# Layer two's mixing: P1 as seven half-depth products, and block sums on GpSimd instead of DMA

## The chip, the cores and the metric

The kernel runs on one core of one Trainium2 chip. The metric is the device time of the whole program in microseconds, the median of several runs of one build. An engine-by-engine profile of one execution stands beside it. The engines are called as in the profile: PE (TensorE, with its weight loads as PEld), DVE (VectorE), ACT (ScalarE), POOL (GpSimd), SP (SyncE, which here only issues DMAs).

## The reference

Four blocks follow each other on a 2048 x 512 activation, each with a layernorm in front and a residual around it: attention, mixer, attention, mixer, all with the same two sets of weights. Attention and the first mixer are called layer one here, the other two layer two. The change lies in the mixer's mixing over the sequence:

```python
def _B_ref(x, w_in, w_sp, b_sp, w_out):      # x: 1 x 2048 x 512, float32
    z = _gelu(jnp.einsum("bsd,df->bsf", x, w_in))      # 2048 x 1792
    z1 = z[..., :Fh]                                   # Fh = 896
    z2 = _layernorm(z[..., Fh:], axis=-1)
    g = jnp.einsum("ts,bsf->btf", w_sp, z2) + b_sp[None, :, None]   # w_sp: 2048 x 2048
    return jnp.einsum("bsf,fd->bsd", z1 * g, w_out)
...
x = x + _A_ref(_layernorm(x, axis=-1), A_wqkv, A_wo)
x = x + _B_ref(_layernorm(x, axis=-1), B_w_in, B_w_sp, B_b_sp, B_w_out)
x = x + _A_ref(_layernorm(x, axis=-1), A_wqkv, A_wo)
x = x + _B_ref(_layernorm(x, axis=-1), B_w_in, B_w_sp, B_b_sp, B_w_out)
```

`w_sp` is the same in both layers, so sums of its blocks that layer one makes can be kept in device memory for layer two.

## The kernel before

**Precision.** Each float32 matrix is split into a high part (`h`, rounded by ACT to the format that PE multiplies) and a low part (`l`, the difference, made by DVE). A product is three matmuls: high by high, high by low, low by high.

**The mixing as seven products.** `g` is computed as a product of 2 x 2 blocks in seven block products instead of eight. Class `P4` does them in the order `P2, P1, P6, P7, P4, P5, P3`. A plain product runs over `k` = 0 to 7; each step takes one tile of 128 x 2 x 512 of the spatial weights (or of a sum of blocks of them), and does 24 matmuls of 128 x 512. A product named in `DIVIDED` for its layer (index 0 is layer one) is itself done as seven products of half depth: 14 steps (`k` = 0 to 13, `SEVEN` gives the order), each of 12 matmuls of 128 x 512. Before the change layer one divides P2 and P4, layer two P2, P4 and P5.

**One step.** For step `g`, `fetch` loads the raw weights from DRAM, five steps ahead, into half a `qd` tile (`Halves` hands those out). `wsp` lets ACT write the high part into a `qd` tile `w` (line 1695), and DVE the low part (line 1698, 128 x 1024 elements); there are six `qd` tiles for both uses. `zsp` (plain) or `zsum` and `zpart` (divided) prepare the z side on ACT and DVE. The weights are made two steps ahead of `mm`, which issues the matmuls. In a divided product `evac_div` adds the finished PSUM banks into the gate tiles `gb` (`unit(n, f)` is 128 x 512 of them) on DVE after every second step (line 1870); in a plain one `evac` does it at the end. Each engine works through its own instructions in the order in which the program writes them; semaphores join the engines. What stands in the program's loop

```python
self.sp(g + 2)
self.zahead(g + (3 if p == "P5" else 4))
self.mm(g)
```

therefore sets the order on every engine. `gate` multiplies finished units by `z1`, part of them on POOL (line 1961). In layer two the low parts of P5 and of half of P7 are not made anew: layer one stores them (`KEPT`), and POOL's queue loads them.

**Sums of weight blocks.** Products of sums need sums of blocks of `w_sp`. `Sums` makes the first level (`s1`, `s`) on POOL during layer one (line 1604); eight of these additions fall into layer one's P1. The second level, for divided products, lies in DRAM tiles `halves[p, m, q]`, with m from 1 to 4. For P2 the sums are made by DVE and POOL; for P4 and P5 by DMA: `halve` copies one block from DRAM to DRAM (SP's queue) and then adds another onto it by an accumulating DMA (POOL's queue, line 1572). P5's copies are issued in layer one's P3 (`PARTS`), its additions in layer one's output stage and in layer two's attention.

**The z side of P1 in layer two.** Column sums of z for P6, P7 and later products, `a[:, H2]`, are made by DVE in `zsp` while P1 runs (lines 1735 and 1736, 128 x 384 each, for 8 tiles).

Of the kernel before, what the change touches and what calls it, by code (L numbers as in the profile page):

```python
# [10 lines left out]
F32 = mybir.dt.float32  # L11
# [84 lines left out]
DIVIDED = ("P2", "P4"), ("P2", "P4", "P5")  # L96
# [17 lines left out]
PARTS |= {("P7", k): 12 + k for k in range(4)} | {("P3", k): 16 + k for k in range(8)}  # L114
# [38 lines left out]
def mixer_kernel(ctx: ExitStack, tc: tile.TileContext, x_in, wqkv, wo_d, win1_d, win2_d, wsp_d, bsp_d, wout_d,  # L153
# [299 lines left out]
    class P1:  # L453
# [1075 lines left out]
    class Sums:  # L1529
# [3 lines left out]
        def __init__(self):  # L1533
# [8 lines left out]
            self.parts, self.halves = [], {}  # L1542
# [4 lines left out]
            self.parts = [(what, p, m, q) for p in ("P4", "P5")[:len(DIVIDED[1]) - 1] for what in ("copy", "add") for m in (1, 3, 2, 4)  # L1547
                          for q in range(2)]
# [7 lines left out]
        def halve(self, n, after, i=None):  # L1556

            if not 0 <= n < len(self.parts):
                return
            what, p, m, q = self.parts[n]  # L1560
            row = 2 if p == "P2" else 0
            j, s = {1: ((1, 0), (1, 4)), 3: ((0, 0), (1, 0)), 2: ((0, 0), None), 4: ((0, 4), None)}[m][what == "add"] or (0, 0)
            src = self.s1[j, s + 2 * q:s + 2 * q + 2] if p == "P5" else wsp_d[row + j, HT + s + 2 * q:HT + s + 2 * q + 2]
            if what == "copy":
                nc.sync.dma_start(self.halves[p, m, q], src)
            else:
                if m in (2, 4):
                    src = self.halves[p, m // 2, q]
                dst = self.halves[p, m, q]
                if i is not None:  # L1570
                    dst, src = dst[i:i + 1], src[i:i + 1]
                d = nc.gpsimd.dma_start(dst, src, accum_op=OP.add, max_dma_last_dim=4096)
                if after is not None:
                    behind(d, after)
# [53 lines left out]
    class P4:  # L1628
# [8 lines left out]
        def __init__(self, p2, sums):  # L1637
# [17 lines left out]
            self.halves, self.fetched = Halves(quads), 0  # L1655

# [5 lines left out]

        def fetch1(self, g):
            p, k = self.steps[g]
            t = self.halves.get()
            if p in self.div:
                r, q = self.SEVEN[k // 2], k % 2
                j, s = {1: (0, 0), 2: (0, 4), 4: (1, 4)}.get(r, (0, 0))
                if r in (1, 2, 4):
                    s += 2 * q  # L1670
                    ap = self.sums.s1[j, s:s + 2] if p == "P5" else wsp_d[(2 if p == "P2" else 0) + j, HT + s:HT + s + 2]
# [18 lines left out]
        def wsp(self, g):  # L1690
# [6 lines left out]
            if at is None or not self.L:  # L1697
                nc.vector.tensor_sub(w[:, 1], r, w[:, 0].bitcast(F32))  # L1698
            if at is not None:
                if self.L:  # L1700
                    nc.gpsimd.dma_start(w[:, 1], at)
                else:
                    nc.sync.dma_start(at, w[:, 1].bitcast(F32))
            self.halves.put(r)
            if g == len(self.steps) - 1:
                self.halves.close()
            self.w[g] = w

        def kept(self, g):
# [3 lines left out]
            if p not in self.div:  # L1713
                t = self.sums.lows[p][:, k]
# [8 lines left out]
        def zsp(self, g):  # L1723
            p, k = self.steps[g]
            H1, H2, H3 = self.H1, self.H2, self.H3
# [41 lines left out]

        def zdiv(self, p, half, side, q, i):
            return ztile[(0 if p == "P5" else HT) + 4 * half + 2 * q + i][:, 256 * side:256 * side + 256]
# [79 lines left out]
        def evac_div(self, p, r):  # L1849
# [4 lines left out]
            for f in range(2):  # L1854
# [6 lines left out]
                n, f = (2 + j if p == "P2" else j), 2 * half + f  # L1861
# [9 lines left out]
            if r in (2, 3, 4):  # L1871
                b = self.bank.pop(name)
                if p != "P5":
# [8 lines left out]
        def carry(self, j):  # L1882
# [3 lines left out]
            nc.scalar.activation(b, self.unit(j, 6), AF.Copy, scale=-1.0)  # L1886
# [77 lines left out]
        def evac(self, p, js=(0, 1)):  # L1964
# [3 lines left out]
            for j in js:  # L1968
                a, b = 2 + j, j
                for f in range(3):  # L1970
# [6 lines left out]
                    elif p == "P6":  # L1977
                        V.tensor_add(self.unit(a, 4 + f), q, bs[a])
                    elif p == "P7":
                        V.tensor_sub(self.unit(b, 4 + f), bs[b], q)  # L1980
# [182 lines left out]
        def out7(self, nxt):  # L2163
# [5 lines left out]
            for j in range(HT):  # L2169
# [76 lines left out]
        def run(self, nxt):  # L2246
# [33 lines left out]
            for g in range(n):  # L2280
# [7 lines left out]
                self.mm(g)  # L2288
                if evac_first:
# [10 lines left out]
                if p in self.div:  # L2300
# [3 lines left out]
                    if k % 2 == 1:  # L2304
                        self.evac_div(p, self.SEVEN[k // 2])
                    if div_first:
# [3 lines left out]
                    if p == "P5":  # L2310
                        if k > 10 and k < 13:
                            self.carry(12 - k)
# [99 lines left out]
```

## Time and profile before

| | |
|---|---|
| median of 3 runs | 1345.41 us (1345.4 to 1346.75) |
| span of the profiled execution, first to last instruction | 1345.0 us |
| PE busy | 1338.2 us, 99% |
| DVE busy | 1043.7 us, 78% |
| ACT busy | 726.6 us, 54% |
| POOL busy | 462.6 us, 34% |
| layer one's P1, P5 on PE | about 385 to 429 us, 532 to 575 us |
| layer two's P2, P1 on PE | 1013 to 1052 us, 1052 to 1095 us |

The profile gives one execution; its span leaves out what lies around the first and the last instruction, so the profiled execution's own time is its span of 1345.0 us and a little more, and the runs' median is 0.4 us above it. A row of the order of time reads: start, length, engine, line, operation, output <- inputs, shapes, count, and in brackets the idle time before it with what ended it. A tile's name without its number: `qd` are weights, `pg` pages of 128 x 512, `bank` is PSUM, `bg` the gate tiles, `z_z` the z tiles. In rows of waits stand the waiting instruction, what it waited for, total us, times, longest. In groups stand count | busy us, mean ns | idle us before.

### The profile page before, as it was taken

Reading aid. Unit: us, or ns where it says so; the run is one execution under the profiler, and the core shown is the slowest. Engines: PE = TensorE matmul, PEld = TensorE weight load, DVE = VectorE, ACT = ScalarE, POOL = GpSimd, SP = SyncE. Lnnn points to the kernel's source line nnn. Section 1 sums busy time; section 2 is a strip of 40 time slices with the busy share of each in tenths; the row PEclk is TensorE's granted clock in tenths of the full one; section 3 lists DMA queues with packets and bytes.
Section 4 is the critical chain, followed back from the end, with each engine's and each line's share of the span. In section 5 each row is a group of like instructions: output and inputs, shape, how many; then the busy total and the mean of one; then the engine's idle time right before and its main releaser. Section 6 shows DMA issues by size and latency. Waiting matters only on the chain.

```text
span 1345.0 us, 19202 instructions
## 1 busy us (share of the span) xinstructions
PE 1338.2 (99%) x6538; PEld 1141.4 (85%) x6538; DVE 1043.7 (78%) x1662; ACT 726.6 (54%) x1219; POOL 462.6 (34%) x613
## 2 busy tenths in 40 slices
PE   9999999999999999999999999999999999999998
PEld 7888888888888888889988888888888888888898
DVE  7679877763797789888867777778689858899885
ACT  5774534334643264445677755557677433666454
POOL 3755675544022300301425543544531012121021
PEclk9999999999999999999999999999999999999999
DMA  5897477877877986884867652678777445579343
GB/s 184 279 318 272 164 262 254 293 270 258 298 236 256 285 265 203 293 306 80 179 172 230 173 133 89 208 238 272 217 206 231 168 168 178 177 241 313 122 79 64
DMA packets 172403, 290.30 MB, mean 216 GB/s; under 512 B 14480, under 2 KB 53904, under 8 KB 172048
## 3 DMA queue, kind: packets, MB, share of 16 engines
q1 hardware_dynamic: 154192, 251.58, 55.5%
q0 software_dynamic: 18112, 37.49, 13.0%
q8 instruction: 51, 0.84, 0.2%
q14 instruction: 48, 0.39, 0.1%
HBM read 204.08 MB, written 101.71 MB: 227 GB/s over the span
## 4 chain that ended last, share of the span: by engine, by line
PE 96%; DMA 1%; DVE 1%; ACT 1%; SPq 0%; issue 0%; POOL 0%; DVEq 0%
PE bank L228 14%; PE bank L230 14%; PE bank L229 13%; PE bank L1920 12%; PE bank L1921 12%; PE bank L1922 12%; PE bank L2118 3%; PE bank L2119 3%; PE bank L2120 3%; PE bank L986 1%; PE bank L988 1%; PE bank L987 1%; DMA pg<-yt 1%; PE bank L384 1%; PE bank L2132 1%; PE bank L2131 1%
## 5 line engine op out<-in xcount | busy, mean ns | idle before, releaser
L1921 PE MATMUL bank<-qd,pg 128*128 128x512 f32 x736 | 286.5, 389 | 0.0
L1920 PE MATMUL bank<-qd,pg 128*128 128x512 f32 x736 | 286.4, 389 | 0.0
L1922 PE MATMUL bank<-qd,pg 128*128 128x512 f32 x736 | 286.3, 389 | 0.0
L1695 ACT ACTIVATE qd<-qd 128x1024 fp32r<-128x1024 f32 x142 | 149.4, 1053 | 127.3 <-PE bank L1922 107.0
L1698 DVE TENSOR_TENSOR qd<-qd,qd 128x1024 fp32r<-128x1024 f32 x132 | 169.2, 1284 | 52.6 <-ACT qd L1695 41.7
L230 PE MATMUL bank<-qd,pg 128*128 128x512 f32 x448 | 174.6, 390 | 0.0
L1921 PEld LDWEIGHTS bank<-qd,pg 128*128 128x128 f32 x736 | 138.2, 188 | 28.9 <-DVE qd L1698 0.3
L1920 PEld LDWEIGHTS bank<-qd,pg 128*128 128x128 f32 x736 | 138.2, 188 | 28.7 <-DVE bg L1870 0.2
L1922 PEld LDWEIGHTS bank<-qd,pg 128*128 128x128 f32 x736 | 138.2, 188 | 28.7
L228 PE MATMUL bank<-qd,pg 128*128 128x512 f32 x308 | 120.6, 392 | 0.3 <-DVE pg L217 0.3
L1961 POOL TENSOR_TENSOR bg<-bg,pg 128x512 f32<-128x512 f32 x28 | 45.7, 1632 | 218.1 <-ACT qd L1695 99.4
L229 PE MATMUL bank<-qd,pg 128*128 128x512 f32 x308 | 120.1, 390 | 0.0
L230 PEld LDWEIGHTS bank<-qd,pg 128*128 128x128 f32 x448 | 84.1, 188 | 17.8 <-DVE pg L217 0.2
L363 POOL TENSOR_SCALAR rs<-mv 128x1 f32<-128x1 f32 x80 | 25.1, 314 | 190.0 <-DVE mv L361 181.0
L372 ACT ACTIVATE pg<-pg,nb,rs 128x512 f32<-128x512 f32 x52 | 42.2, 812 | 85.5 <-POOL nb L366 79.3
L1604 POOL TENSOR_TENSOR pg<-pg,pg 128x512 f32<-128x512 f32 x48 | 68.0, 1417 | 59.2 <-DMA pg<-in_wsp_dram 57.3
L214 ACT ACTIVATE pg<-pg 128x512 fp32r<-128x512 f32 x85 | 53.0, 624 | 61.7 <-DVE pg L1789 18.4
L2120 PE MATMUL bank<-wo,qd 128*128 128x256 f32 x288 | 81.4, 283 | 0.0
L2118 PE MATMUL bank<-wo,qd 128*128 128x256 f32 x276 | 78.2, 283 | 0.0
L2119 PE MATMUL bank<-wo,qd 128*128 128x256 f32 x276 | 78.0, 283 | 0.0
L228 PEld LDWEIGHTS bank<-qd,pg 128*128 128x128 f32 x308 | 57.9, 188 | 12.5 <-DVE pg L217 0.7
L229 PEld LDWEIGHTS bank<-qd,pg 128*128 128x128 f32 x308 | 58.0, 188 | 12.1 <-DVE qd L217 0.2
(276 smaller groups left out, 3278.6 us busy)
## 6 DMA issues: line engine op xcount, KB each, us to landing
qd<-s SPq DMA_DIRECT2D x62, 512.0 KB, 4.2
qd<-in_wsp_dram SPq DMA_DIRECT2D x40, 512.0 KB, 4.1
qd<-hP SPq DMA_DIRECT2D x40, 512.0 KB, 4.7
pg<-z SPq DMA_DIRECT2D x56, 256.0 KB, 4.9
pg<-in_wsp_dram SPq DMA_DIRECT2D x52, 256.0 KB, 4.3
s<-pg SPq DMA_DIRECT2D x48, 256.0 KB, 3.7
z<-pg SPq DMA_DIRECT2D x40, 256.0 KB, 3.3
pg<-w POOLq DMA_DIRECT2D x38, 256.0 KB, 4.6
```

What stands on the lines that cost most here:

```text
L228: nc.tensor.matmul(out, ah, bh, start=start, stop=False)
L229: nc.tensor.matmul(out, ah, bl, start=False, stop=False)
L230: nc.tensor.matmul(out, al, bh, start=False, stop=stop)
L1604: nc.gpsimd.tensor_tensor(t, a, b, op=OP.add)
L1695: self.mark = nc.scalar.activation(w[:, 0], r, AF.Copy)
L1698: nc.vector.tensor_sub(w[:, 1], r, w[:, 0].bitcast(F32))
L1920: m(out, h[:, o], w[:, 0, j, :], start=start, stop=False, skip_group_check=True)
L1921: m(out, h[:, o], w[:, 1, j, :], start=False, stop=False, skip_group_check=True)
L1922: m(out, l[:, o], w[:, 0, j, :], start=False, stop=stop, skip_group_check=True)
L2118: m(out, A, x, start=start and f == 0, stop=False, skip_group_check=True)
L2119: m(out, A, y, start=False, stop=False, skip_group_check=True)
L2120: m(out, B, x, start=False, stop=stop and f == 2, skip_group_check=True)
```

## The change

1. P1 joins the divided products of layer two: 14 steps of 12 matmuls instead of 8 of 24. Its results are added into units by `evac_div`; the starting values that P6, P7 and `carry` need come from four new POOL sums (`base`).
2. The block sums that this needs (`halves["P1", ...]`), and those of P5, which DMAs made, are made by POOL in layer one's P1 and P5: these go through their weights in pairs (`PAIRED`), keep both raw tiles of a pair, and `pairsums` adds them, four sums of 128 x 512 a pair, sixteen a product. `pairstore` writes each to DRAM from SP's queue. The sums lie in gate tiles (P1) or in z tiles that are no longer needed (P5) until stored. P5's part of `halve` goes.
3. In layer two's P2 and P1 each third low part of the weights is made by POOL instead of DVE.
4. The column sums of z in layer two move from DVE (`zsp`) to POOL (`hsum`), one instruction a step, steps 2 to 17.

```diff
-DIVIDED = ("P2", "P4"), ("P2", "P4", "P5")
+DIVIDED = ("P2", "P4"), ("P2", "P1", "P4", "P5")
+PAIRED = (0, 4, 1, 5, 2, 6, 3, 7)
...
-PARTS |= {("P7", k): 12 + k for k in range(4)} | {("P3", k): 16 + k for k in range(8)}
+PARTS |= {("P7", k): 12 + k for k in range(4)}
...
-                    if 9 <= s < NT + 1:
-                        sums.halve(28 + (s - 9) // 2, None, (s - 9) % 2)
...
+        def paired(self, p):
+
+            return not self.L and p in ("P1", "P5")
+
+        def block(self, p, k):
+            return PAIRED[k] if self.paired(p) else k
...
-            if at is None or not self.L:
+            p, k = self.steps[g]
+            if self.L and p in ("P2", "P1") and g % 3 == 1:
+                nc.gpsimd.tensor_tensor(w[:, 1], r, w[:, 0].bitcast(F32), op=OP.subtract)
+            elif at is None or not self.L:
                 nc.vector.tensor_sub(w[:, 1], r, w[:, 0].bitcast(F32))
...
+            if self.paired(p):
+                self.pairsums(g, r)
+                return
             self.halves.put(r)
...
+        def pairsums(self, g, r):
+
+            p, k = self.steps[g][0], self.block(*self.steps[g])
+            self.rest[k] = r
+            if k < 4:
+                return
+            k -= 4
+            x, y = self.rest.pop(k), self.rest.pop(k + 4)
+            a, b, c, d = x[:, 0], x[:, 1], y[:, 0], y[:, 1]
+            n = 4 * (k % 2)
+            if p == "P1":
+                o = [self.unit(k % 2, f) for f in range(4)]
+            else:
+                o = [ztile[HT + n + f][:, 0:512] for f in range(4)]
+            for t, u, v in zip(o, (b, b, a, c), (d, a, o[0], o[2])):
+                nc.gpsimd.tensor_tensor(t, u, v, op=OP.add)
+            self.halves.put(x)
+            self.halves.put(y)
+            self.due.append((g, p, k, o))
+
+        def pairstore(self, g):
+
+            while self.due and self.due[0][0] <= g:
+                _, p, k, o = self.due.popleft()
+                for m, t in zip((1, 3, 2, 4), o):
+                    nc.sync.dma_start(self.sums.halves[p, m, k // 2][k % 2], t)
...
+        def hsum(self, n):
+
+            k, m = divmod(n, 2)
+            if 0 <= k < HT:
+                a, b, H1, H2 = ztile[k], ztile[k + HT], self.H1, self.H2
+                x, y, op = (a[:, H2], b[:, H2], OP.add) if m else (a[:, H1], a[:, H2], OP.subtract)
+                nc.gpsimd.tensor_tensor(a[:, H2], x, y, op=op)
+
+        def base(self, j, fresh):
+
+            u, b = self.unit(2 + j, 2), self.bs[2 + j if fresh else j]
+            nc.gpsimd.tensor_tensor(self.unit(2 + j if fresh else j, 6), b, u, op=OP.subtract if fresh else OP.add)
...
-        def carry(self, j):
+        def carry(self, p, j):
...
+            if p == "P1":
+                nc.scalar.activation(b, self.unit(2 + j, 2), AF.Copy)
...
                     elif p == "P6":
-                        V.tensor_add(self.unit(a, 4 + f), q, bs[a])
+                        own = f == 2 and "P1" in self.div
+                        V.tensor_add(self.unit(a, 4 + f), q, self.unit(a, 4 + f) if own else bs[a])
...
-                    if j < 4:
-                        self.sums.halve(24 + j, None)
...
                 self.mm(g)
+                self.pairstore(g)
+                if "P1" in self.div:
+                    self.hsum(g - 2)
...
+                    if p == "P2" and "P1" in self.div and k in (9, 11):
+                        for fresh in (True, False):
+                            self.base(k == 9, fresh)
```

Three places in the order of instructions. The line numbers are those of each kernel, so the changed kernel's differ: its DVE low part is line 1705, its POOL low part 1703, `pairsums` 1734, `hsum` 1812, `base` 1817, its first-level sums 1597, its gate products 2017.

POOL in layer one's P1, before: eight first-level sums, then the gate products of P1.

```order
L1604 TENSOR_TENSOR pg_425_4261<-pg_424_4259,pg_425_4261 128x512
L1604 TENSOR_TENSOR pg_424_4259<-pg_424_4259,pg_426_4263 128x512
L1604 TENSOR_TENSOR pg_426_4263<-pg_425_4261,pg_426_4263 128x512
L1604 TENSOR_TENSOR pg_429_4299<-pg_426_4263,pg_429_4299 128x512
L1604 TENSOR_TENSOR pg_433_4341<-pg_432_4339,pg_433_4341 128x512
L1604 TENSOR_TENSOR pg_432_4339<-pg_432_4339,pg_434_4343 128x512
L1604 TENSOR_TENSOR pg_434_4343<-pg_433_4341,pg_434_4343 128x512
L1604 TENSOR_TENSOR pg_437_4383<-pg_434_4343,pg_437_4383 128x512
L1961 TENSOR_TENSOR bg_9_3891<-bg_9_3891,pg_446_4500 128x512
```

The same stretch of POOL in the changed kernel, up to the third pair (`bg` 7 and 8 are the gate tiles that hold the sums):

```order
L1734 TENSOR_TENSOR bg_7_3897<-qd_19_3770 128x512 x2
L1734 TENSOR_TENSOR bg_7_3897<-qd_19_3770,bg_7_3897 128x512 x2
L1734 TENSOR_TENSOR bg_8_3898<-qd_18_3682 128x512 x2
L1734 TENSOR_TENSOR bg_8_3898<-qd_18_3682,bg_8_3898 128x512 x2
L1597 TENSOR_TENSOR pg_425_4274<-pg_424_4272,pg_425_4274 128x512
L1597 TENSOR_TENSOR pg_424_4272<-pg_424_4272,pg_426_4276 128x512
L1597 TENSOR_TENSOR pg_426_4276<-pg_425_4274,pg_426_4276 128x512
L1597 TENSOR_TENSOR pg_429_4320<-pg_426_4276,pg_429_4320 128x512
L1734 TENSOR_TENSOR bg_7_3897<-qd_35_4201 128x512 x2
L1734 TENSOR_TENSOR bg_7_3897<-qd_35_4201,bg_7_3897 128x512 x2
```

Eight sums of two pairs stand ahead of the old ones, and eight more between and behind them.

POOL in layer two, before: from the last stores ahead of the mixing straight to the gate products that follow P1.

```order
L1145 DMA z_1_3_1_10426<-bg_22_10223 128x512
L1145 DMA z_1_3_2_10429<-bg_22_10223 128x512
L1961 TENSOR_TENSOR bg_25_10482<-bg_25_10482,pg_1049_11045 128x512
L1961 TENSOR_TENSOR bg_25_10482<-bg_25_10482,pg_1054_11114 128x512
L1961 TENSOR_TENSOR bg_25_10482<-bg_25_10482,pg_1057_11143 128x512
```

The same place in the changed kernel, from the second store to the fifth low part:

```order
L1144 DMA z_1_3_2_10482<-bg_22_10276 128x512
L1703 TENSOR_TENSOR qd_132_10583<-qd_126_10271,qd_132_10583 128x1024
L1812 TENSOR_TENSOR z_z_8597<-z_z_8597 128x384
L1812 TENSOR_TENSOR z_z_8597<-z_z_8597,z_z_9564 128x384
L1812 TENSOR_TENSOR z_z_8693<-z_z_8693 128x384
L1703 TENSOR_TENSOR qd_135_10660<-qd_127_10401,qd_135_10660 128x1024
...
L1703 TENSOR_TENSOR qd_138_10733<-qd_127_10401,qd_138_10733 128x1024
L1812 TENSOR_TENSOR z_z_8882<-z_z_8882 128x384
L1812 TENSOR_TENSOR z_z_8882<-z_z_8882,z_z_9835 128x384
L1817 TENSOR_TENSOR bg_26_10536<-pg_980_10293,bg_26_10536 128x512
L1817 TENSOR_TENSOR bg_24_10534<-pg_978_10289,bg_26_10536 128x512
```

In all 9 low parts, 16 column sums and 4 `base` sums have come in between, in POOL's queue in the order of the steps.

DVE in layer one's P6, before (the first number in a name is the buffer): the low parts go round four `qd` buffers, 2 to 5.

```order
L1698 TENSOR_TENSOR qd5_45_4574<-qd1_18_3674,qd5_45_4574 128x1024
L1762 SCALAR_TENSOR_TENSOR pg15_453_4578<-z3_z0_2255,pg20_452_4577 128x384
L1698 TENSOR_TENSOR qd2_46_4604<-qd0_19_3762,qd2_46_4604 128x1024
L1762 SCALAR_TENSOR_TENSOR pg9_456_4608<-z4_z0_2390,pg2_455_4607 128x384
L1698 TENSOR_TENSOR qd3_47_4634<-qd0_19_3762,qd3_47_4634 128x1024
L1762 SCALAR_TENSOR_TENSOR pg18_459_4638<-z5_z0_2529,pg19_458_4637 128x384
L1698 TENSOR_TENSOR qd4_48_4664<-qd1_18_3674,qd4_48_4664 128x1024
```

The same rows in the changed kernel:

```order
L1705 TENSOR_TENSOR qd5_46_4615<-qd3_35_4201,qd5_46_4615 128x1024
L1800 SCALAR_TENSOR_TENSOR pg15_453_4619<-z3_z0_2263,pg20_452_4618 128x384
L1705 TENSOR_TENSOR qd2_47_4645<-qd0_19_3770,qd2_47_4645 128x1024
L1800 SCALAR_TENSOR_TENSOR pg9_456_4649<-z4_z0_2398,pg2_455_4648 128x384
L1705 TENSOR_TENSOR qd4_48_4675<-qd0_19_3770,qd4_48_4675 128x1024
L1800 SCALAR_TENSOR_TENSOR pg18_459_4679<-z5_z0_2537,pg19_458_4678 128x384
L1705 TENSOR_TENSOR qd5_49_4705<-qd1_18_3682,qd5_49_4705 128x1024
```

Buffer 3 now holds raw weights (it stands on the right), and the low parts go round 2, 4 and 5.

More of the change, by code (lines that the diff above doesn't have):

```diff
@@ L1541, in __init__ @@
             self.groups, self.adds, self.made2 = deque(range(4)), (deque(), deque()), []
[L1542 removed]
+            self.halves = {}
             for p in DIVIDED[1]:
@@ L1546, in __init__ @@
                         self.halves[p, m, q] = dram.tile([2, P, 512], F32, name=f"h{p}_{m}_{q}")
-            self.parts = [(what, p, m, q) for p in ("P4", "P5")[:len(DIVIDED[1]) - 1] for what in ("copy", "add") for m in (1, 3, 2, 4)
-                          for q in range(2)]
+            self.parts = [(what, m, q) for what in ("copy", "add") for m in (1, 3, 2, 4) for q in range(2)]
         def fetch(self):
@@ L1713, in kept @@
             if p not in self.div:
-                t = self.sums.lows[p][:, k]
+                t = self.sums.lows[p][:, self.block(p, k)]
             else:
@@ L1860, in evac_div @@
                                       3: (0, 1, -1, False), 4: (1, 0, 1, True)}[r]
-                n, f = (2 + j if p == "P2" else j), 2 * half + f
+                n, f = (2 + j if p in ("P2", "P1") else j), 2 * half + f
+                if p == "P1":
+                    new = False
                 if p == "P4" and f < 3:
```

48 lines of the change are left out of this document (29 added, 19 removed).

## The prediction

> **What bounds the kernel now.** I read the page first (busy shares, then the chain that ended last), then PE's waits, then the engines by stretch, and last the order of time on DVE and GpSimd (POOL).
>
> ```profile
> span 1345.0 us, 19202 instructions
> PE 1338.2 (99%) x6538; PEld 1141.4 (85%) x6538; DVE 1043.7 (78%) x1662; ACT 726.6 (54%) x1219; POOL 462.6 (34%) x613
> ...
> PE 96%; DMA 1%; DVE 1%; ACT 1%; SPq 0%; issue 0%; POOL 0%; DVEq 0%
> ```
>
> ```profile
> PE bank L617 <- DVE pg L612: 2.3, 1, 2.3
> PE bank L1153 <- ACT bank L1170: 0.4, 1, 0.4
> PE bank L228 <- DVE pg L217: 0.3, 1, 0.3
> ```
>
> These are all of PE's waits in the whole span, 3.0 us (total, times, longest). So each matmul that goes is a gain of its issue time, and each microsecond by which another engine falls behind PE is a loss. Three starts of PE fix the price of a matmul: the first of layer two's P2, of its P1, of its P6.
>
> ```profile
> 1013.19 0.39 PE L1920 MATMUL bank<-qd,pg 128*128 128x512 f32 x1
> ...
> 1051.55 0.39 PE L1920 MATMUL bank<-qd,pg 128*128 128x512 f32 x1
> ...
> 1095.07 0.39 PE L1920 MATMUL bank<-qd,pg 128*128 128x512 f32 x1
> ```
>
> P1 is 8 steps of 24 matmuls: 43.52 us / 192 = 0.2267 us each, 5.44 a step. P2, already seven products, is 14 steps of 12: 38.36 us, 2.72 a step.
>
> Next, how far the other engines are from PE's pace. The stretches are layer one's P1 and P5, then layer two's P2 and P1; the columns are length, then busy time of PE, PEld, DVE, ACT, POOL.
>
> ```profile
> 385.00:429.00 44.00, 44.00 (x196) 36.45 (x195) 34.36 (x38) 13.91 (x18) 13.40 (x8) 1.00 0.87 299
> 531.70:575.20 43.50, 43.50 (x194) 36.03 (x193) 34.81 (x50) 18.31 (x28) 12.11 (x6) 1.00 0.80 274
> 1013.20:1051.50 38.30, 38.30 (x169) 31.40 (x168) 36.49 (x60) 26.14 (x40) 2.06 (x4) 1.00 0.75 246
> 1051.50:1095.00 43.50, 43.50 (x193) 36.02 (x193) 26.91 (x39) 12.34 (x16) 1.29 (x1) 1.00 0.41 141
> ```
>
> In layer two's P2, DVE is busy 36.5 of 38.3 us: it only just keeps up, and POOL is next to idle there. In P1 DVE has 16 us to spare. The change makes P1 a second P2 and fills POOL in both.
>
> **DVE and POOL exclude each other.** Layer one's P1, DVE in order of time (start, length):
>
> ```profile
> 391.37 0.55 DVE L1735 TENSOR_TENSOR z_z<-z_z 128x384 f32<-128x384 f32 x1
> 391.96 0.56 DVE L1736 TENSOR_TENSOR z_z<-z_z,z_z 128x384 f32<-128x384 f32 x1
> 392.44 0.68 DVE L1760 TENSOR_TENSOR pg<-z_z,pg 128x512 fp32r<-128x512 f32 x1
> 393.04 1.22 DVE L1698 TENSOR_TENSOR qd<-qd,qd 128x1024 fp32r<-128x1024 f32 x1
> 394.17 1.65 DVE L1735 TENSOR_TENSOR z_z<-z_z 128x384 f32<-128x384 f32 x1
> 395.86 1.53 DVE L1736 TENSOR_TENSOR z_z<-z_z,z_z 128x384 f32<-128x384 f32 x1
> 397.31 1.77 DVE L1760 TENSOR_TENSOR pg<-z_z,pg 128x512 fp32r<-128x512 f32 x1
> 399.01 2.31 DVE L1698 TENSOR_TENSOR qd<-qd,qd 128x1024 fp32r<-128x1024 f32 x1
> 401.24 0.55 DVE L1735 TENSOR_TENSOR z_z<-z_z 128x384 f32<-128x384 f32 x1
> ```
>
> and POOL beside it, four sums back to back:
>
> ```profile
> 393.48 6.75 POOL L1604 TENSOR_TENSOR pg<-pg,pg 128x512 f32<-128x512 f32 x4 [53.73 <-DMA pg<-in_wsp_dram]
> ```
>
> Alone, the four DVE instructions of a step take 394.17 - 391.37 = 2.80 us. Beside the four sums they take 401.24 - 394.17 = 7.07. So each 128x512 sum holds DVE up for (7.07 - 2.80) / 4 = 1.07 us, and the two engines take turns. An operand in PSUM is exempt:
>
> ```profile
> 1091.87 4.09 DVE L1975 TENSOR_TENSOR bg<-bg,bank 128x512 f32<-128x512 f32 x6 [4.69 <-PE bank L1922]
> ```
> ```profile
> 1092.69 1.29 POOL L1961 TENSOR_TENSOR bg<-bg,pg 128x512 f32<-128x512 f32 x1 [77.44 <-DVE bg L1975]
> ```
>
> Six evacuations in 4.09 us with a POOL product in their midst: 0.68 each, no wait. That POOL row also says that POOL had stood idle 77 us, so layer two's P2 and P1 never met this exclusion before.
>
> [...]
>
> **The change part by part.** *Matmuls.* Layer two's P1 goes from 192 to 14 x 12 = 168: 24 x 0.2267 = **-5.4 us**. Certain, as long as PE stays fed.
>
> *Prices on DVE and POOL.* From layer two's P2, starts without POOL beside them, and POOL's own records by shape:
>
> ```profile
> 1029.69 0.75 DVE L1787 TENSOR_TENSOR pg<-z_z,z_z 128x256 f32<-128x256 f32 x2
> 1030.36 0.68 DVE L217 TENSOR_TENSOR pg<-pg,pg 128x512 fp32r<-128x512 f32 x1
> 1030.96 1.22 DVE L1698 TENSOR_TENSOR qd<-qd,qd 128x1024 fp32r<-128x1024 f32 x1
> 1032.10 0.68 DVE L217 TENSOR_TENSOR pg<-pg,pg 128x512 fp32r<-128x512 f32 x1
> 1032.70 1.28 DVE L1870 TENSOR_TENSOR bg<-pg,bank 128x512 f32<-128x512 f32 x2
> 1033.90 1.22 DVE L1698 TENSOR_TENSOR qd<-qd,qd 128x1024 fp32r<-128x1024 f32 x1
> ```
> ```profile
> L222 POOL TENSOR_TENSOR bg<-pg,bg 128x512 fp32r<-128x512 f32 x7 | 9.1, 1295 | 1.3 <-ACT bg L214 1.3
> L740 POOL TENSOR_TENSOR qd<-qd 128x256 f32<-128x256 f32 x12 | 10.3, 862 | 0.7
> ```
>
> Start to start, a low half (L1698) costs DVE 1.14 us, an evacuation 0.60. No POOL op of 128x1024 or 128x384 is shown. By the slope of the two records, 0.433 us per 256 columns, 1024 would hold 1.07 + 0.87 = 1.94 us; by twice the whole record, 2.59. I take twice the hold, 2.14, the 512 row being the nearest and its hold the quantity that counts; 384 columns by proportion 0.80. [...]
>
> *Layer two's P2.* Off DVE: 5 low halves (every third step), 5.7 us, so 36.5 - 5.7 = 30.8 stay. On POOL: 5 low halves (10.7), 12 of the 16 column sums `hsum` (9.6), 4 `base` sums (4.3): 24.6. Together 55.4 for a stage of 38.1: 17.3 short if nothing overlaps, 10.1 if all 12 evacuations (7.2) run under POOL work. *P1 as seven*: DVE as in P2 less 4 low halves, 31.9; POOL 4 x 2.14 + 4 x 0.80 = 11.8; together 43.7 against 38.1: 5.6 short, or nothing. The 16 column operations of the old P1 (L1735, L1736) leave DVE but come back as `hsum`, and the eight-fold evacuation at its end becomes twelve smaller ones, counted in the 31.9. So 10 to 23. I take **+20**, near the upper end: evacuations come in pairs of 1.2 us after every second step and cover only a sum that waits just then; and POOL's low halves queue behind `hsum` and `base` on POOL, so PE waits for POOL too.
>
> *Layer one's P1.* Sixteen new POOL sums of 128x512 (`pairsums`) beside the 8 old ones. DVE's 34.4 busy us hold 8 x 1.07 of waits already; 16 x 1.07 = 17.1 more make 51.5 for 44.0: **+7.5**. Bounds 0 (DVE runs ahead, and the old eight cost PE nothing) and 9.8 (24 sums, 4 a step, 6 steps of 7.07 against 5.44 us, no lead).
>
> *Layer one's P5.* Likewise 34.8 + 17.1 = 51.9 for 43.5: 8.4. Raw halves are kept until their pair is there, so from P1 on the `w` tiles go round three buffers instead of four, as the order of DVE in P6 shows, which shortens DVE's lead. **+8**; bounds 0, and 12 with 3 for SP's queue (below) and the lost buffer.
>
> *DMAs.* Off SP 8 copies, off POOL's queue 12 accumulating DMAs of this row:
>
> ```profile
> L1572 POOL DMA_DIRECT2D hP<-hP x12 | 9.8, 819 | 16.2 <-ACT qd L1695 16.2
> ```
>
> PE waited for none, so 0. On SP: 32 stores of 256 KB, 6 more loads of 512 KB. A store waits in SP's queue for POOL's sum and holds the raw loads behind it; they are asked five steps ahead (27 us in layer one), against some 5 us of sums, so 0 in the sum. Layer two's loads: DMA is busy 0.41 of P1, so the 6 fit.
>
> *Sum*: -5.4 + 20 + 7.5 + 8 = +30.1. The profiled execution spans 1345.0; the runs' median is 1345.41, 0.4 above it. 1345.4 + 30.1 = 1375.5, say **1376**. Lower end: -5.4 + 10 + 3.5 + 3 (half of layer one under DVE's lead) = +11, 1356. Upper: -5.4 + 27 (23 and nine times 0.45, with 1024 at 2.59 us) + 9.8 + 12 = +43, 1389, say 1390.
>
> **Rivals.** *Faster*: POOL's work fits into what DVE leaves, PE never waits: 1340. For it stands that the eight old sums at 393 us cost PE nothing. It decides at the price of a sum: P2 has 7.5 us of room, 14.7 with the evacuations, for the worth of 23 sums of 128x512, so one would have to hold DVE for 0.33 to 0.64 us instead of 1.07. Against it stand four turns in a row in the rows above. *Layer two only*: DVE's lead swallows layer one's sums, as it did the eight: 1345.4 - 5.4 + 20 = 1360. Against: the lead is spent once, and 16 sums follow it twice. *POOL itself the path*: its low halves come later than all sums queued before them, and each PE step behind one waits for a whole POOL queue: some 2 us for each of nine beyond the sum, 1394. *No change* (1343 to 1348) needs stalls that happen to equal 5.4. That the change doesn't do what it says is excluded by the order of instructions.
>
> **Chances.** The forecast (1366 to 1390) 0.70; layer two only (1350 to 1366) 0.12; POOL the path (over 1390) 0.07; faster 0.08; no change 0.03. 0.2% is 2.7 us, about what a measurement of this kernel can tell. Slower thus 0.89. Range 1356 to 1390, which leaves out the faster and unchanged cases, the far upper one, and the mildest of layer two only.
>
> **What would show it.** PE 24 matmuls fewer, but a list of waits of some 35 us: on DVE's low half in both layers, on POOL's in layer two. In layer two's P2 and P1, spans of about 52 and 44 instead of 38 us, DVE's low half stretched from 1.22 towards 2 to 3 us wherever a POOL row overlaps, its evacuations at 0.68. In layer one, P1 and P5 51 us instead of 43.5. I am wrong if DVE keeps its 1.22 us beside POOL, if a 1024-wide POOL sum turns out cheap, or if the waits sit in layer two alone.

## The result, and the profile after

The changed kernel takes 1386.69 us, median of 4 runs (1385.7 to 1387.2); the kernel before, on the same chip, 1346.08 (1345.4 to 1348.4). The ratio is 1.0298, 95% interval 1.0285 to 1.0310: 40.6 us slower, where 30 were forecast. The page of the changed kernel begins so, and its chain reads so:

```profile
span 1385.0 us, 19320 instructions
...
PE 1349.5 (97%) x6514; PEld 1140.8 (82%) x6514; DVE 1101.4 (80%) x1675; ACT 738.0 (53%) x1241; POOL 564.8 (41%) x662
...
PE 82%; DVE 11%; issue 2%; DMA 2%; ACT 2%; SPq 0%; POOL 0%; DVEq 0%; ACTq 0%; POOLq 0%
```

PE has its 24 matmuls fewer, and yet its busy time grew by 11 us, from 1338.2: some matmuls have become slower. PE's waits, 3.0 us in all before, now are, the largest of them (line, releaser; total, times, longest):

```profile
PE bank L1977 <- DVE qd L1705: 13.7, 10, 3.6
PE bank L1976 <- DVE bg L1923: 3.7, 1, 3.7
PE bank L1976 <- ACT wo L215: 3.6, 1, 3.6
...
PE bank L1978 <- DVE pg L1798: 2.2, 5, 0.9
PE bank L1976 <- ACT pg L1796: 2.2, 2, 1.9
PE bank L1977 <- POOL qd L1703: 1.7, 1, 1.7
```

L1705 is DVE's low half, that is its low part of the weights of a step (L1698 before), L1703 POOL's. The `...` stands for the 2.3 us at the program's start, which were there before. Next, the stages by PE's starts, layer one's P1, P4, P5, P3, then layer two's P2, P1 (columns as in the prediction: length, PE, PEld, DVE, ACT, POOL, PE's clock, DMA share):

```profile
389.90:441.60 51.70, 46.24 (x193) 36.88 (x192) 46.85 (x40) 12.43 (x16) 33.97 (x20) 0.97 0.94 336
506.90:546.30 39.40, 38.62 (x169) 31.44 (x168) 35.90 (x57) 25.36 (x37) 9.66 (x4) 1.00 0.54 171
546.30:600.00 53.70, 47.41 (x193) 36.44 (x192) 45.06 (x50) 18.07 (x29) 31.95 (x19) 0.97 0.81 276
600.00:633.40 33.40, 33.34 (x144) 27.63 (x145) 28.91 (x48) 13.18 (x21) 0.00 (x0) 0.95 0.47 164
1035.60:1085.20 49.60, 41.84 (x170) 32.13 (x168) 48.13 (x55) 24.32 (x40) 29.70 (x20) 0.97 0.54 184
1085.20:1134.70 49.50, 42.53 (x169) 33.42 (x168) 48.65 (x59) 24.98 (x38) 21.75 (x13) 0.93 0.53 173
```

| Stage | before, us | after, us | difference |
|---|---|---|---|
| layer one P1 | 43.5 | 51.7 | +8.2 |
| layer one P4 | 38.1 | 39.4 | +1.3 |
| layer one P5 | 43.5 | 53.7 | +10.2 |
| layer one P3 | 31.7 | 33.4 | +1.7 |
| layer two P2 | 38.4 | 49.6 | +11.2 |
| layer two P1 | 43.5 | 49.5 | +6.0 |

Together +38.6; the rest of the 40 us of span is some 1 us outside these stages (1.8 more ahead of layer one's P1, 0.9 less between the two mixings). Lengths run from the first matmul of a stage to that of the next; so taken, P1 and P5 of layer one lay at 388.1 to 431.6 and 534.9 to 578.5 us before, some 3 us later than the windows that the prediction shows for them.

The engines take turns as forecast. First DVE, then POOL in layer one's P1:

```profile
393.50 1.64 DVE L1773 TENSOR_TENSOR z_z<-z_z 128x384 f32<-128x384 f32 x1
395.18 1.50 DVE L1774 TENSOR_TENSOR z_z<-z_z,z_z 128x384 f32<-128x384 f32 x1
396.61 1.75 DVE L1798 TENSOR_TENSOR pg<-z_z,pg 128x512 fp32r<-128x512 f32 x1
398.27 1.27 DVE L1923 TENSOR_TENSOR bg<-pg,bank 128x512 f32<-128x512 f32 x2
399.47 1.21 DVE L1705 TENSOR_TENSOR qd<-qd,qd 128x1024 fp32r<-128x1024 f32 x1
```
```profile
392.46 3.80 POOL L1734 TENSOR_TENSOR bg<-qd,bg 128x512 f32<-128x512 f32 x2
396.23 7.15 POOL L1597 TENSOR_TENSOR pg<-pg,pg 128x512 f32<-128x512 f32 x4
```

The first three DVE instructions, each with two SBUF inputs, are 0.9 to 1.1 us longer than alone (0.55, 0.56, 0.68); the two evacuations from PSUM, in the midst of POOL's sums, are not (1.27 for two). Here the one that started first went first: the low half at 399.47 started 0.09 us ahead of the third of POOL's four sums and took its 1.21 us, and that sum took 2.25, where a sum alone takes 1.29.

**What the prediction did not have** is in PE's row. PE waits 3.67 us, and after that issues at 0.427 us instead of 0.227:

```profile
394.94 0.39 PE L1978 MATMUL bank<-qd,pg 128*128 128x512 f32 x1
399.00 0.74 PE L1976 MATMUL bank<-qd,pg 128*128 128x512 f32 x1 [3.67 <-DVE bg L1923]
399.54 0.63 PE L1977 MATMUL bank<-qd,pg 128*128 128x512 f32 x1
399.96 0.63 PE L1978 MATMUL bank<-qd,pg 128*128 128x512 f32 x1
```

until 402.5 us ("half rate" from here on). The column of the granted clock, in windows cut where it changes, says the same:

```profile
392.27:395.69 3.42, 3.06 (x14) 2.20 (x12) 3.39 (x3) 0.00 (x0) 3.34 (x3) 1.00 1.05 401
395.69:399.10 3.41, 0.10 (x1) 0.10 (x1) 3.41 (x4) 0.00 (x0) 3.33 (x3) 1.00 0.86 330
399.10:402.51 3.41, 3.41 (x8) 2.68 (x9) 3.38 (x4) 0.60 (x1) 3.25 (x3) 0.50 0.70 213
402.51:405.93 3.42, 3.42 (x16) 2.82 (x15) 3.42 (x3) 0.98 (x2) 3.42 (x3) 1.00 0.99 280
```

A window of 3.41 us in which PE was idle, and then one at clock 0.50, in which 8 matmuls start instead of 15 or 16: 1.71 us of work lost. The trace has six such stretches: one in each of layer one's P1, P5 and P3 and layer two's P2, two in layer two's P1; 10.2 us. The 38.6 us are thus -5.4 (matmuls) + 33.8 (waits) + 10.2 (half rate). The waits are what is left in this sum; PE's starts, as far as they lie more than 0.227 us apart at full clock, give 34 us. The list of waits has some 27 in these stages, because it counts only from a matmul's end, 0.39 us after its start.

### The profile page after: what moved, and what is told of

It reads as the page before. It is cut to its first block, busy times and chain, and to the rows that moved or that the text cites. A ratio compares the mean times of both kernels' runs of the same rounds, so it can differ in the third digit from the quotient of the medians.

```text
span 1385.0 us, 19320 instructions
## 1 busy us (share of the span) xinstructions
PE 1349.5 (97%) x6514; PEld 1140.8 (82%) x6514; DVE 1101.4 (80%) x1675; ACT 738.0 (53%) x1241; POOL 564.8 (41%) x662
## 3 DMA queue, kind: packets, MB, share of 16 engines
q0 software_dynamic: 16896, 33.30, 11.2%
## 4 chain that ended last, share of the span: by engine, by line
PE 82%; DVE 11%; issue 2%; DMA 2%; ACT 2%; SPq 0%; POOL 0%; DVEq 0%; ACTq 0%; POOLq 0%
PE bank L231 13%; PE bank L230 13%; PE bank L229 13%; PE bank L1977 8%; PE bank L1978 8%; PE bank L1976 8%; DVE qd L1705 3%; PE bank L2176 3%; PE bank L2177 3%; PE bank L2178 3%; PE bank L985 1%; PE bank L986 1%; PE bank L987 1%; DVE bg L1923 1%; DVE pg L1798 1%
## 5 line engine op out<-in xcount | busy, mean ns | idle before, releaser
L1977 PE MATMUL bank<-qd,pg 128*128 128x512 f32 x728 | 288.5, 396 | 15.5 <-DVE qd L1705 13.7
L1976 PE MATMUL bank<-qd,pg 128*128 128x512 f32 x728 | 287.7, 395 | 9.5 <-DVE bg L1923 3.7
L1699 ACT ACTIVATE qd<-qd 128x1024 fp32r<-128x1024 f32 x148 | 155.6, 1052 | 121.1 <-PE bank L1978 98.2
L1705 DVE TENSOR_TENSOR qd<-qd,qd 128x1024 fp32r<-128x1024 f32 x129 | 174.5, 1355 | 47.3 <-ACT qd L1699 47.3
L1977 PEld LDWEIGHTS bank<-qd,pg 128*128 128x128 f32 x728 | 138.9, 191 | 49.1 <-DVE qd L1705 17.9
L1976 PEld LDWEIGHTS bank<-qd,pg 128*128 128x128 f32 x728 | 139.1, 191 | 40.9 <-DVE bg L1923 4.1
L1978 PEld LDWEIGHTS bank<-qd,pg 128*128 128x128 f32 x728 | 138.8, 191 | 34.5 <-DVE pg L1798 5.7
L215 ACT ACTIVATE pg<-pg 128x512 fp32r<-128x512 f32 x93 | 58.1, 625 | 104.4 <-DVE pg L1840 26.1
L231 PEld LDWEIGHTS bank<-qd,pg 128*128 128x128 f32 x448 | 84.1, 188 | 18.2 <-DVE pg L218 0.4
L2017 POOL TENSOR_TENSOR bg<-bg,pg 128x512 f32<-128x512 f32 x28 | 51.9, 1852 | 73.5 <-ACT qd L1699 64.7
L218 DVE TENSOR_TENSOR pg<-pg,pg 128x512 fp32r<-128x512 f32 x91 | 71.1, 782 | 3.3 <-ACT pg L215 3.2
L229 PEld LDWEIGHTS bank<-qd,pg 128*128 128x128 f32 x308 | 57.8, 188 | 12.5 <-ACT pg L215 0.6
```

Source lines behind the costliest of these rows:

```text
L218: nc.vector.tensor_sub(l, src, h.bitcast(F32))
L229: nc.tensor.matmul(out, ah, bh, start=start, stop=False)
L231: nc.tensor.matmul(out, al, bh, start=False, stop=stop)
L1699: self.mark = nc.scalar.activation(w[:, 0], r, AF.Copy)
L1976: m(out, h[:, o], w[:, 0, j, :], start=start, stop=False, skip_group_check=True)
L1977: m(out, h[:, o], w[:, 1, j, :], start=False, stop=False, skip_group_check=True)
```

## The experiments

The theory: POOL's new sums hold DVE up, DVE's low halves come late, PE waits, and after a long wait runs at half rate for a while. The rivals: the waits come from the new order (stores behind POOL in SP's queue, a buffer fewer) or from POOL's queue, and the half rate from something else than PE's idleness. Ratios are to the kernel before, on the same chip.

**1. Without the new POOL sums: in both layers (but for 64 of the 384 columns of `hsum`), in layer one, in layer two.**

```
e_l1:   pairsums:  nc.scalar.activation(t, u, AF.Copy)                for  nc.gpsimd.tensor_tensor(t, u, v, op=OP.add)
e_l2:   wsp:       nc.scalar.activation(w[:, 1], r, AF.Copy)          for  POOL's low half
        base:      nc.scalar.activation(..., u, AF.Copy)              for  POOL's sum
        hsum:      ... a[:, H2][:, 0:64], x[:, 0:64], y[:, 0:64] ...  on POOL
e_both: both
```

> All the POOL sums that the change added are replaced: the sixteen-and-sixteen sums of layer one and the 5 + 4 low halves and 4 base sums of layer two by plain copies on ACT (same outputs, same stores, same buffers), hsum narrowed from 384 to 64 columns. Left out: the sums themselves, so the values are not the kernel's. Exclusion (POOL sums hold DVE up): PE's 24 matmuls fewer are all that is left, 1346.1 - 5.4 = 1340.7, between 1339 and 1344, no half-rate stretch of PE. Rival 'order' (the stores in SP's queue, the lost buffer, the new order of DVE's work cost the time): still over 1370.

> Layer one alone without POOL sums: its 32 pair sums become ACT copies of one operand (left out: the addition); stores, buffers and all of layer two as in the changed kernel. In the changed kernel's trace layer one shows 14.6 us of extra PE waits and three half-rate stretches of some 1.7 us. Exclusion: these go, 1386.7 - 19.9 = 1367, between 1364 and 1370, with three half-rate stretches left, all in layer two. Rival 'order' (SP's stores and the lost buffer): 1380 to 1387. Rival 'layer two only': 1387.

> Layer two alone without POOL's new work: low halves and base sums become ACT copies, hsum narrowed to 64 columns (left out: these operations); layer one as in the changed kernel. Exclusion: the 26.6 us that layer two shows (21.4 of waits, three half-rate stretches of some 1.7) go: 1360, between 1357 and 1364, three half-rate stretches left, all in layer one. If the two layers did not simply add, e_l1 and e_l2 together would give back more or less than e_both.

Measured: e_both 1346.07 us, ratio 0.9997 (0.9987 to 1.0006); e_l1 1366.83, 1.0157 (1.0142 to 1.0172); e_l2 1362.81, 1.0126 (1.0111 to 1.0141). So the new POOL work carries all of the loss (1386.7 - 1346.1 = 40.6), roughly in halves: 19.9 us in layer one, as expected, and 23.9 in layer two. PE's waits in e_l1:

```profile
PE bank L1977 <- DVE qd L1705: 13.7, 10, 3.6
...
PE bank L1977 <- POOL qd L1703: 1.7, 1, 1.7
PE bank L1976 <- DVE bg L2045: 1.4, 1, 1.4
```

The 13.7 us on DVE's low half are there unchanged, 13 of them in layer two and 0.8 in layer one's P4. Of layer one's other waits 1.4 us at the end of P5 are left, and of the six stretches of half rate the three of layer two. e_l1 and e_l2 give back 43.8 us together, 3 more than e_both, but the layers don't act on each other: by the traces the stages of the mixing give back 18.4 us in e_l1, 22.8 in e_l2 and 41.1 in e_both. The rest lies ahead of layer one's P1, where the four kernels do the same: PE gets there at 389.9 us in the changed kernel and at 390.0 in e_both, but at 387.5 and 387.6 in e_l1 and e_l2.

e_both misses its 1339 to 1344. The gain of 5.4 is there in layer two's P1, 38.2 us instead of 43.5, but not in the total: layer one's P4 and P5 are 1.3 and 1.7 us longer than before, with a wait of 0.8 us in P4 and one of 1.5 at the end of P5 (the release L1976 <- L2045), and PE got to layer one's P1 1.9 us later than in the trace before. e_l1, without POOL sums in layer one, has both waits too. They belong to the new order or to the copies; P4's was not taken apart. e_both's runs spread from 1343.7 to 1347.9.

P5's can be followed in the traces, and in the changed kernel it is one of the three longest waits, the 3.6 us that the list puts down to ACT. SP's queue, then DVE and PE there:

```profile
587.47 0.37 SPq L1710 DMA_DIRECT2D lowP<-qd  x1
587.89 2.71 SPq L1744 DMA_DIRECT2D hP<-z_z  x4
592.06 0.89 SPq L197 DMA_DIRECT2D pg<-in_wout_dram  x2
```
```profile
597.10 0.42 DVE L2074 TENSOR_TENSOR pg<-pg 128x256 f32<-128x256 f32 x1 [2.15 <-DMA pg<-in_wout_dram]
599.23 3.07 DVE L2045 TENSOR_TENSOR bg<-bg,bank 128x512 f32<-128x512 f32 x5
```
```profile
600.05 0.47 PE L1976 MATMUL bank<-qd,pg 128*128 128x512 f32 x1 [3.59 <-ACT wo L215]
```

The store of a low half (`lowP`) stood at the head of SP's queue for 8.5 us, until DVE's late low half was done; the four stores of pair sums took 2.7 us more; and only then were the output weights (`in_wout_dram`) asked for, 4 us before P5's last matmul, where before the change it was 11. DVE waited for them, first 2.15 and then 0.57 us, and its evacuation of P5's results (L2045) comes behind, the one that e_both's and e_l1's lists name as PE's release. In e_both and e_l1 DVE waits there as well (1.1 and 0.5, 1.0 and 0.6 us), and PE 1.5 and 1.4. So this wait reaches PE through SP's queue, and POOL's sums lengthen it.

**2. Late POOL or held DVE?** Only the low halves are taken off POOL (the wsp line of e_l2 alone), so PE waits for no POOL product in P2 and P1.

> As the changed kernel, but layer two's 9 POOL low halves are ACT copies (left out: the subtraction); hsum and base stay on POOL in full width, and PE waits for none of them in P2 or P1. Exclusion: DVE's 30.8 us in P2 with 12 x 0.80 + 4 x 1.07 us of holds make 44.7 for 38.1, so 6.6 us stay, and perhaps one half-rate stretch: 1367 to 1370 with layer one's 19.9. Rival 'POOL itself the path' (PE waits because POOL's low halves come late in POOL's queue): nothing is left in layer two, 1360.

Measured: 1375.83 us, 1.0221 (1.0206 to 1.0237). The rival's 1360 is excluded: 13 us more than e_l2 stay, with waits on DVE. In the changed kernel PE waits for POOL's low half once, 1.7 us. How the 10.9 us that went divide between POOL's lateness and its holds of DVE, this run can't tell. DVE beside hsum, in the list of DVE's instructions in layer two's P2:

```profile
1038.92 2.39 DVE L1836 TENSOR_TENSOR pg<-z_z,pg 128x256 f32<-128x256 f32 x2
1041.23 1.50 DVE L218 TENSOR_TENSOR pg<-pg,pg 128x512 fp32r<-128x512 f32 x1
...
1046.35 2.01 DVE L1705 TENSOR_TENSOR qd<-qd,qd 128x1024 fp32r<-128x1024 f32 x1
```

Each instruction is 0.8 us over its time alone (0.75 for the first two together, 0.68, 1.22): the price of hsum's 384 columns was right. My 1367 to 1370 were too low all the same: P2 lost 7.8 us, of which 5.1 are one wait and the rest two windows of half rate, and P1 4.7 where I had nothing: DVE enters P1 without any lead (it is busy without a gap from 1081 to 1094 us), so its few holds there count in full. Layer one's wait at the end of P5 was longer too, 5.2 us.

**3. Reading, or being busy?** In layer one each sum becomes two writes of the same tile.

```
pairsums:  nc.gpsimd.memset(t, 0.0)   (twice)   for  nc.gpsimd.tensor_tensor(t, u, v, op=OP.add)
```

> As the changed kernel, but each of layer one's 32 pair sums on POOL becomes two memsets of its 128x512 destination on POOL (left out: the sums): POOL stays occupied and writes SBUF, but reads nothing. If DVE is held up because both engines read two operands from SBUF, the memsets hold nobody: 1367, as with the sums on ACT (1366.8), DVE's low half at 1.22 us beside them. If any work of POOL on SBUF holds DVE, or POOL's lateness makes the waits: 1380 to 1390, according to the memsets' length.

Measured: 1369.71 us, 1.0172 (1.0157 to 1.0187); with ACT's copies it was 1366.8. POOL's rows, and DVE's beside them:

```profile
398.51 0.53 POOL L1734 MEMSET bg<- 128x512 f32 x1
...
401.69 6.84 POOL L1597 TENSOR_TENSOR pg<-pg,pg 128x512 f32<-128x512 f32 x4
```
```profile
398.53 0.55 DVE L1774 TENSOR_TENSOR z_z<-z_z 128x384 f32<-128x384 f32 x1
399.11 0.56 DVE L1775 TENSOR_TENSOR z_z<-z_z,z_z 128x384 f32<-128x384 f32 x1
399.59 0.68 DVE L1799 TENSOR_TENSOR pg<-z_z,pg 128x512 fp32r<-128x512 f32 x1
400.19 1.22 DVE L1705 TENSOR_TENSOR qd<-qd,qd 128x1024 fp32r<-128x1024 f32 x1
401.32 0.55 DVE L1774 TENSOR_TENSOR z_z<-z_z 128x384 f32<-128x384 f32 x1
401.91 1.53 DVE L1775 TENSOR_TENSOR z_z<-z_z,z_z 128x384 f32<-128x384 f32 x1
```

Two memsets occupy POOL 1.05 us per sum, as long as a sum holds DVE, and DVE runs at its full pace beside them; at 401.7 POOL's old sums begin, and DVE is slow again at once. So in this run it was POOL's reading of SBUF that held DVE up, not its being busy or its writing: DVE's low half took 1.22 us beside the memsets, and 2.31 beside an old sum at 396.30 us. Whether reading one input is enough, no run shows. The 2.9 us over e_l1 (2.0 by the ratios, since the two ran on different chips) are mostly a longer wait at the end of P5 (2.6 us instead of 1.4) with a half-rate stretch behind it: DVE waits there for the output weights again, 1.6 and 1.2 us.

**4. The half rate by itself**, in the kernel before, with no POOL work added: DVE's low half is repeated in `wsp`.

```
for _ in range(HOLD.get((self.L, *self.steps[g]), 1)):
    nc.vector.tensor_sub(w[:, 1], r, w[:, 0].bitcast(F32))
st_lump:  HOLD = {(0, "P5", 4): 14, (1, "P1", 4): 16}
st_even:  HOLD = {(1, "P1", k): 4 for k in range(1, 8)}
```

> The kernel before, without the change, with one of DVE's low halves written many times over at two places (14 times at P5's block 4 in layer one, 16 times at P1's block 4 in layer two), so that PE waits once some 8 to 12 us and once some 4 to 7 us with no POOL work in it. Theory 'half rate': after each of these waits PE issues at 0.427 us a matmul for 3.4 or 6.8 us, 1.6 to 2.6 us lost each, the clock list shows two stretches of 0.5, and the time is before + waits + 3 to 5. Rival: the slow matmuls in the changed kernel come from POOL and DVE sharing SBUF; then none here, before + waits.

> The kernel before with the low half of blocks 1 to 7 of P1 in layer two written four times each: 21 low halves more, 24 us of DVE work, spread over the stage. PE waits some 7 us in all, in pieces of 1 to 1.7 us. Theory 'half rate': no piece is long enough, clock 1.0 throughout, the time is before + 7 and nothing more (1352 to 1355). Rival (each wait costs a fixed restart): a loss beside each of the pieces.

Measured: st_lump 1371.29 us, 1.0183 (1.0170 to 1.0197); st_even 1354.40, 1.0056 (1.0043 to 1.0069). In st_lump PE waits some 20 us at the two places, and the time is 24.6 longer: 4 to 5 for half rate. Its second wait, in windows on the same grid:

```profile
1089.57:1092.98 3.41, 0.00 (x0) 0.00 (x0) 3.31 (x4) 0.14 (x1) 0.00 (x0) 1.00 0.00 0
1092.98:1096.40 3.42, 0.80 (x1) 0.29 (x1) 3.35 (x6) 0.00 (x0) 0.00 (x0) 0.50 0.20 42
1096.40:1099.81 3.41, 3.40 (x8) 2.72 (x9) 3.38 (x5) 0.00 (x0) 0.00 (x0) 0.50 0.65 201
1099.81:1103.20 3.39, 3.39 (x16) 2.81 (x16) 3.35 (x6) 0.00 (x0) 0.00 (x0) 1.00 0.69 208
```

POOL is at zero in all of them, so the rival falls: PE's idleness alone is enough. st_even, with waits of 2.7, 0.9 and four of 1.0 us (7.6 in all), took 7.75 us more and shows one clock throughout:

```profile
1051.00:1105.00 54.00, 47.35 (x202) 37.26 (x201) 53.04 (x63) 13.34 (x18) 1.30 (x1) 1.00 0.34 113
```

**5. The seven products without the POOL sums.** If the exclusion is all, P1 in seven products should pay when its sums are made elsewhere. The core of it, against the kernel before:

```
-DIVIDED = ("P2", "P4"), ("P2", "P4", "P5")
+DIVIDED = ("P2", "P4"), ("P2", "P1", "P4", "P5")
-KEPT = ("P7", "P5")
+KEPT = ("P7", "P5", "P1")
+PARTS |= {("P4", k): 32 + k for k in range(8)}       # the 8 copying DMAs for P1
 e4 (layer two):  + V.tensor_sub(a[:, H2], a[:, H1], a[:, H2])    # hsum, first half, in the attention
 zsp, P6:         + V.tensor_add(a[:, H2], a[:, H2], b[:, H2])    # hsum, second half
 base:            ACT copies in P2, DVE sums in P6
 the 8 accumulating DMAs (one adds a 512 KB block sum in DRAM):
   v_dma           output stage of layer one, and layer two's attention (740 to 780 us)
   v_p5, v_p5b     layer one's P5; P7's first four low halves kept as well
   v_late, v_late2 layer two's attention, in halves; low halves as in v_p5
```

> The seven products in layer two's P1 without any of the new POOL sums. Undone: the pair sums, the POOL low halves, hsum on POOL, base on POOL. Instead P1's block sums are made by 8 copying and 8 accumulating DMAs in layer one's P4 and output stage and layer two's attention, as P5's were; hsum's work is done by DVE, 9 of 16 operations in layer two's attention, where DVE is busy 0.65 to 0.8, the rest in P6; base by ACT copies in P2 and DVE in P6; P1's low halves are stored in layer one and loaded in layer two. The whole is computed. Exclusion theory: 24 matmuls fewer and waits of some 2 us: 1342, between 1340 and 1345. Rival: 4 MB more of stores in layer one's P1, where DMA is busy 0.87, make PE wait for its loads: 1346 to 1355.

> As v_dma, with its three visible losses taken out: the 8 accumulating DMAs go from the output stage and layer two's attention (some 5 us of PE waits there) to layer one's P5; hsum's additions are all in P6 (0.8 us of wait in the attention); P7's first four low halves are stored in layer one and loaded too (1.4 us of waits in P7). The whole is computed. Exclusion theory: 24 matmuls fewer and about 1 us of waits, 1342, between 1340.5 and 1345, faster than before by 0.1 to 0.45%. Rival: the stores and accumulating DMAs, 10 MB more in layer one's P4 to P7, now make PE wait for loads there: 1345 to 1352.

> As v_p5, but one of hsum's eight additions stays in layer two's attention: 0.7 us of wait there as in v_dma, against up to 0.5 us at the start of P6. Expected within 1 us of v_p5.

> As v_p5b, but P1's 8 accumulating DMAs are cut into halves of 256 KB and spread over layer two's attention (8 of them beside P5's, 8 in its second part), away from layer one's P5, where DMA was busy 1.00 and PE waited, and away from the output stage. The whole is computed. From v_p5b's layer two (4.7 us gained from P2 on) and its layer one up to P4 (0.8 us of wait): 1346.6 - 4.7 + 0.8 + 0 to 2 in the attention = 1343 to 1345, faster by 0.1 to 0.3%. Rival: POOL's issues of accumulating DMAs (0.9 us each) in the attention make DVE and PE wait as in v_dma, 0.5 us each: 1347 to 1351.

> As v_late, but all 16 halves are issued in the second part of layer two's attention, one in each step, behind P5's. Expected within 1 us of v_late; if the first part is the sensitive one, as v_dma's waits at 740 to 780 us suggest, this one is the faster: 1342 to 1344.

| Kernel | median, us | ratio | interval |
|---|---|---|---|
| v_dma | 1350.49 | 1.0030 | 1.0019 to 1.0041 |
| v_p5 | 1354.96 | 1.0063 | 1.0050 to 1.0076 |
| v_p5b | 1354.54 | 1.0057 | 1.0044 to 1.0071 |
| v_late | 1345.42 | 0.9985 | 0.9976 to 0.9994 |
| v_late2 | 1348.67 | 1.0014 | 1.0005 to 1.0023 |

Three of the five missed: v_dma, v_p5 and v_late2, which should have been the faster of its pair. (v_late lies 0.4 us above its 1343 to 1345, on a chip where the kernel before is 0.5 us slower.) In v_dma layer one's P1 ran at a DMA share of 1.02 without a wait of PE, so the rival's place was wrong, but PE waits about 5 us more than before where the accumulating DMAs were put, a third of it where layer one's output is added. v_late has the same column sums in the attention and waits about 1 us there, so the DMAs' size and place is the likely cause. In v_p5 DMA is at 1.00 in P5 and P3, and now PE does wait, long enough for half rate (a window over the end of P5 and P3):

```profile
575.00:608.00 33.00, 30.07 (x120) 24.26 (x120) 27.80 (x49) 17.34 (x31) 2.45 (x3) 0.90 1.00 325
```

v_late, the best of five placements, is 1.7 us under the kernel before (1347.1 beside it), less than the 0.2% that I set as the limit; its interval excludes no change, barely. v_late2 lost its 3 us against v_late between the two mixings, where its 16 halves lie (407.1 us instead of 404.0). v_late's longest waits in the mixing, of both layers (the first is mostly layer one's P4, the second layer two's P1):

```profile
PE bank L1953 <- DVE qd L1714: 0.9, 2, 0.8
...
PE bank L1863 <- ACT qd L1711: 0.4, 1, 0.4
```

So the seven products can be had without loss, and the 24 matmuls are worth less than 2 us once the work around them is paid for: in v_late's trace layer two's P1 is 5.3 us shorter, and layer one's P4 1.2, layer two's P2 0.7 and the stretch between the mixings 0.9 longer.

## Why the prediction was right or wrong

- *Matmuls, -5.4*: right; 6514 instead of 6538, and layer two's P1 without POOL work (e_both) takes 38.2 us instead of 43.5.
- *The exclusion, 1.07 us per 512 columns*: right, with the exempt PSUM operand. It was argued from eight old sums; experiment 3 shows that it hangs on POOL's reading.
- *POOL's low half of 1024 columns, 2.14*: right as a hold. DVE's low half beside one, in layer two's P2, lasts 2.1 us longer than 1.22:

```profile
1053.52 3.32 DVE L1705 TENSOR_TENSOR qd<-qd,qd 128x1024 fp32r<-128x1024 f32 x1
```
```profile
1053.42 2.34 POOL L1703 TENSOR_TENSOR qd<-qd,qd 128x1024 fp32r<-128x1024 f32 x1 [2.31 <-ACT qd L1699]
```

- *Layer one's P1, +7.5*: it lost 8.2, of which 1.7 are half rate; 6.5 of waits.
- *Layer one's P5, +8*: P5 and P3 lost 11.9, of which 3.4 are half rate; 8.5 of waits, close to the forecast, but not all by its mechanism: the last wait, 3.6 us, came through SP's queue. P4's 1.3 was not in the sum.
- *Layer two, +20*: 11.2 + 6.0 + 5.4 = 22.6, of which 5.1 are half rate; 17.5 of waits. The forecast's spans of 52 and 44 us came out as 49.6 and 49.5: I had given P1 little, but P2's lag goes on into it.
- *DMAs and SP's queue, 0*: wrong in part. PE's list has no wait for raw weights, but the output weights behind the stores came late: the 3.6 us at the end of P5 and the half rate after them, 5.3 us in all, some 1.5 of it also without POOL's sums. P4 and P5 together lose 3 us in e_both. (The twelve accumulating DMAs that went are eight of the row shown and four of `hP<-s`; the sum is the same.)
- *The step that failed* is the one from waits to time. I forecast 35.5 us of waits, and there were 33.8; but I wrote that each microsecond by which another engine falls behind PE is a loss of one, and it was 1.3: the 10.2 us of half rate were missing. The trace before has a sign of it at the program's start alone, where PE's first eight matmuls start 0.427 us apart (2.9 to 5.5 us); after that PE never waited over 0.4 us there, so no row priced a long wait.
- *The range*: the forecast's mechanism and most of its terms held, but that 1386.7 lies inside owes something to luck. The upper end allowed for 27, 9.8 and 12 us of waits, where 17.5, 6.5 and 8.5 came; the half rate, which no bound had, filled that room.
- *Rivals*: layer two only (1360) is refuted by e_l1, which gave back 19.9 us; POOL itself the path (1394) is nearest in time, but e_low refutes it as the main mechanism; faster (1340) would need holds that are not held.

## What to carry to other kernels

Before moving a sum from a busy DVE to an idle POOL, look for one place in the trace where both run sums from SBUF side by side: if they take turns there, count what a sum holds as DVE's time (here 1.07 us for 128x512). What lay beside POOL's sums for free here was DVE's PSUM work (two evacuations in 1.27 us) and ACT's work (its high part of 128x1024 took 1.04 to 1.07 us beside them and without them). When PE is the bound, price a wait by its length: the six of 0.9 to 2.7 us in st_even, 7.6 us together, cost 7.75, and the one of 3.67 us in the changed kernel's P1 brought 1.71 us of half rate on top, about half as much again. When stores of late results go into a queue, look at which loads stand behind them. A saving in matmuls is worth what remains after DVE's slack in that stage is spent, so read DVE's busy time in the stage itself first.

## What the runs showed of the hardware

**Half rate came on a fixed grid.** In the changed kernel's trace all changes of the granted clock lie multiples of 3.413 us apart (399.10 and 590.25 us are 56 of them apart, 590.25 and 1057.87 are 137). From PE's starts in six traces (the changed kernel, e_l1, e_l2, e_low, e_set, st_lump) I took PE's idle time in each window of that grid in the mixing and the attention. After all 21 full-rate windows with 2.03 us or more of idle time, the next window ran at half rate; after those with less, up to 2.01 us, none did. (With the profile's modelled ends of matmuls the line lies between 1.85 and 1.87 us.) In the changed kernel's trace alone six windows have 2.4 to 3.3 us, and half rate follows; the others have 1.3 at most. The eight other traces follow it: v_p5 and v_p5b have one such window each, the rest none. So in these traces it was neither one wait's length nor a wholly idle window that counted, but whether PE stood idle for some 55 to 60% of a window (1.87 us of 3.413 by the modelled ends, 2.03 by PE's starts). A wait of 2.3 us inside one window brought it about in the changed kernel (1085.2 us); one of 2.7 us in e_low that a window's edge cut into 1.3 and 1.4 did not. The half-rate window at 1092.98 us in st_lump, with PE busy for 0.80 of 3.42 us, was followed by another; the six of the changed kernel, in which PE was busy throughout, were not.

**A POOL memset of 128x512 took 0.53 us** in e_set, against 1.30 for a sum of two inputs in the kernel before (L222, seven of them), and DVE ran at its full pace beside it (0.55, 0.56, 0.68 and 1.22 us for the instructions of a step).
